# Transposes of the identity in pairs 1 to 4, and another PSUM bank for the last 64 queries' second scores

## The chip, the cores and the metric

One core of one Trainium2 chip runs the whole program. The metric is the device time of one execution in microseconds (us). Three executions of the kernel before took 951.35, 951.52 and 954.31 us, a median of 951.52 us. The profile is of one more execution, which took 954.08 us; its span, from the first to the last instruction, is 952.4 us.

## What is computed

An attention layer is followed by two feed-forward layers. Cut to what matters here (B, H, S, D = 4, 8, 576, 64):

```python
scores = scale * np.matmul(q, k.transpose(0, 1, 3, 2))          # per batch and head, 576 x 576
scores = np.where(causal, -1e9, scores)
a = np.exp(scores - scores.max(-1, keepdims=True)); a /= a.sum(-1, keepdims=True) + 1e-9
local = np.matmul(a, v)
mem_out = (phi(q) @ M_prev) / (phi(q) . z_prev)
attn = g * mem_out + (1 - g) * local
x = relu(attn @ w_in) ** 2 @ w_out                              # 2304 tokens, 512 -> 2048 -> 512
out = gate[token] * relu(x @ w1[e]) @ w2[e]                     # e: the token's best of 8 experts
```

## The kernel before

The attention walks over 16 pairs (a batch and two heads). A pair has nine units, in the order of `ORDER`: unit 0 is the last 64 queries of both heads (576 keys), units 1 to 8 are the four blocks of 128 queries of head 0 and head 1, in the row order 3, 0, 2, 1. One loop (L611) counts units through all pairs: `t = 9 * pair + i`. In its turn `t` the loop issues, for TensorE in exactly this order, since TensorE's order is the written one (L1458):

- `busy(n)` where `BUSY` lists `t`: n transposes of the identity into a tile `w`, which nobody reads;
- the products with the values (`values`, L538) of unit `t - 8`, into a tile `xo`;
- a step of the first feed-forward layer (`step`, L1445), once enough of its input is there (from pair 5 on);
- the transposes of the next pair's queries and keys (`prep`: `tk`, `tq`, `t2`, `tp`);
- the transposes of unit `t - 5`'s probabilities (`turn`, L500);
- the scores of unit `t` (`scores`, L446), which end in a PSUM tile `ps`.

VectorE masks the scores of unit `t` and takes their maximum in turn `t + 1` (L480, called the reduction below); ScalarE then exponentiates, VectorE inverts the sums (L489 to L495), GpSimd scales (L434, L437). VectorE and GpSimd also convert the feed-forward weights from the float64 bits that DMAs bring (L117), a few operations in nearly every turn, so that VectorE's line holds much that is not attention. Up to turn 71 VectorE's and GpSimd's orders are the written ones too.

PSUM banks: `psS` has two, in turn, for the scores. Unit 0 needs more than a bank's 512 columns and takes two tiles, 320 columns and 256 columns; the second is called the second scores below. `psX` has one bank: `xo`, the sum over the values of a pair's first 512 queries, is opened in the fifth unit of the next pair (i = 5), closed in i = 8, and copied out by ScalarE (L585) in the turn after. `busy` also uses `psX`; before the change it runs only in turns -5 to 7, where no `xo` is open. A tile in a bank can be written only when the bank's earlier tile has been read.

Of the kernel before, what the change touches and what calls it, by code (L numbers as in the profile page):

```python
# [9 lines left out]
F32 = DT.float32  # L10
# [11 lines left out]
B, H, S, D = 4, 8, 576, 64  # L22
# [34 lines left out]
START, EARLY, MIX = (3, 2, 1), 5, 1  # L57

FREE = 72
STRICT, BUSY = 9, {-5: 14, 0: 12, 2: 6, 4: 4, 5: 4, 6: 4, 7: 4}  # L60


TURN0, TURN1 = 5, 3
# [124 lines left out]
def attention(tc, sh, q, k, v, M, z, beta, w_in, w_out, mlp, step):  # L188

    nc = tc.nc  # L190
    with ExitStack() as ctx:
        c = ctx.enter_context(tc.tile_pool(name="ac", bufs=1))
        st = ctx.enter_context(tc.tile_pool(name="ast", bufs=2))
        psS = ctx.enter_context(tc.tile_pool(name="psS", bufs=2, space=PSUM))
        psT = ctx.enter_context(tc.tile_pool(name="psT", bufs=2, space=PSUM))
        psX = ctx.enter_context(tc.tile_pool(name="psX", bufs=1, space=PSUM))
# [39 lines left out]
        def load(p):  # L236
            b, hp = divmod(p, NPP)
            qn_, kn_ = naturals.get(p, (qn, kn))
            fetch(p, (k, kn_), (q, qn_))
            zb = st.tile([128, 128], F32, name="zb", tag="zb")  # L240
            nc.sync.dma_start(zb, z[b:b + 1, 2 * hp:2 * hp + 2].rearrange("o h d -> o (h d)").to_broadcast([128, 128]))
            nat[p] = (vns[p % 3], zb, Mts[p % 3], qn_, kn_)
# [8 lines left out]
        def fetch(p, *pairs):  # L251
            b, hp = divmod(p, NPP)
            for src, t in pairs:
                eng = nc.scalar if p == 0 and src is q else nc.sync
                for h in range(2):
                    eng.dma_start(t[:, 0:4, h * 64:h * 64 + 64],
                                      src[b, 2 * hp + h, 0:512].rearrange("(c p) d -> p c d", p=128))
                eng.dma_start(t[:64, 4].rearrange("p (h d) -> p h d", h=2),
                                  src[b, 2 * hp:2 * hp + 2, 512:576].rearrange("h p d -> p h d"))
# [159 lines left out]
        def new_S(b):  # L419
            if b == 0:  # L420
                turns[0] += 1
                if turns[0] % 3 == 0:
                    return sh.psm.tile([128, 512], F32, name="ps", tag="L1", bufs=1)
            return psS.tile([128, 512], F32, name="ps", tag="S")
# [4 lines left out]
        def scale(p, h, r, n, a, b):  # L429

            if p < NPP:
                d = diag[p, h, r] = diags[:, made[0] % 8 * 128:made[0] % 8 * 128 + 128]
                made[0] += 1
                nc.gpsimd.tensor_scalar(d, ident, a, b, ALU.mult, ALU.mult)  # L434
            else:
                A = soft[p, h, r][:, :n]
                nc.gpsimd.tensor_scalar(A, A, a, b, ALU.mult, ALU.mult)  # L437
# [8 lines left out]
        def scores(p, h, r):  # L446

            qs, ks, hq, lq, hk, kl = state[p][:6]
            qz = state[p][8]
            b, hp = divmod(p, NPP)  # L450
            A = A8 if h is None else st.tile([128, 512 if r > 1 else 256], F32, name="A", tag="A" if r > 1 else "As",
                                              bufs=NA if r > 1 else NAS)
            nm = st.tile([128, 2], F32, name="nm", tag="nm", bufs=5)
            if h == 1:
                sm = sums.pop((p, r))
            else:
                sm = sums[p, r] = st.tile([128, 2], F32, name="sm", tag="sm", bufs=5)
            soft[p, h, r] = A
            if h is None:
                n = S  # L460
                parts = [(0, 320, 320), (320, 256, 256)]
                terms = [(qb[0], hk), (qb[1], hk), (qb[0], kl)]
            else:
                n = 128 * (r + 1)
                parts = [(0, n, max(n, 256))]
                rows, half = slice(r * 128, r * 128 + 128), slice(h * 64, h * 64 + 64)
                if p:
                    terms = [(qs[:, h, rows], ks[:, h]), (qz[:, h, rows], kl)]
                else:
                    terms = [(hq[half, rows], hk[half]), (lq[half, rows], hk[half]), (hq[half, rows], kl[half])]  # L470
            tiles = []
            for a, w, wide in parts:
                ps = new_S(b)
                tiles.append(ps)
                for j, (x, y) in enumerate(terms):
                    nc.tensor.matmul(ps[:, :wide], x, y[:, a:a + wide], start=j == 0, stop=j == len(terms) - 1)  # L476
            yield
            for j, (a, w, _) in enumerate(parts):
                end = 768 if h is not None else 256 if j else 576
                nc.vector.tensor_tensor_reduce(A[:, a:a + w], tiles[j][:, :w], mask[:, end - w:end], -1.0, 3e38,  # L480
                                               ALU.add, ALU.min, nm[:, j:j + 1])
            if len(parts) > 1:
                nc.vector.scalar_tensor_tensor(nm[:, 0:1], nm[:, 0:1], 3e38, nm[:, 1:2], ALU.min, ALU.min)
            yield
            i = h or 0
            nc.scalar.activation(A[:, :n], A[:, :n], AF.Exp, bias=nm[:, 0:1], scale=-1.0, accum_out=sm[:, i:i + 1])  # L486
            yield
            if h is None:
                nc.vector.scalar_tensor_tensor(sm[:, 0:1], sm[:, 0:1], 1e-9, mask[:, 0:1], ALU.add, ALU.add)  # L489
                nc.vector.reciprocal(sm[:, 0:1], sm[:, 0:1])  # L490
                sums.pop((p, r))
                scale(p, h, r, n, sm[:, 0:1], g2[:, hp:hp + 1])
            elif h:
                nc.vector.scalar_tensor_tensor(sm, sm, 1e-9, mask[:, 0:2], ALU.add, ALU.add)
                nc.vector.reciprocal(sm, sm)  # L495
                for i in range(2):
                    scale(p, i, r, n, sm[:, i:i + 1], g1[:, 2 * hp + i:2 * hp + i + 1])
            yield
# [101 lines left out]
        def due(eng):  # L600
            for f in queue.pop((t, eng), ()):
                f()

        def busy(n):

            w = psX.tile([128, 512], F32, name="w", tag="X")
            for _ in range(n):
                nc.tensor.transpose(w[:, :128], ident, ident)

        here, before, gens, t = None, None, [prep(0)], -EARLY  # L610
        while t < len(units) + LP + 5 or queue:  # L611
            now[0] = t
            p, i = divmod(t, 9)
            if t == STRICT:
                strict.close()
                strict.enter_context(tc.manual_schedule(engines={ENG.DVE, ENG.Pool}))
            if t == FREE:
                strict.close()
            if t in BUSY:
                busy(BUSY[t])  # L620
            start = START[min(p, 2)]
            if 0 <= p < NPAIR - 1 and i == start:
                gens.append(prep(p + 1))
            for d, x in evacs:
                nc.scalar.copy(d, x)
            evacs.clear()
            due("act0")
            if here is not None:
                next(here)
            due("dve0")  # L630
            with then(ENG.Activation):
                if here is not None:
                    next(here)
            with then(ENG.DVE):
                if before is not None:
                    next(before)
            before, here = here, None
            if t == MIX:
                mix()
            if t == AHEAD:  # L640
                next(conv)
            due("act")
            with then(ENG.DVE):
                due("dve")
            due("pool")
            if t > CONV[0] and t % 9 != CONV[1] and next(conv, conv) is not conv:
                sh.converted += 1
            n = t - LP
            if n % 9 == 0 and (n - 1) // 9 in JOINED:
                values(*units[n - 1])  # L650
            if 0 <= n < len(units) and (n % 9 < 8 or n // 9 not in JOINED):
                values(*units[n])
            if 0 <= p < NPAIR - 2 and i == 8:
                load_values(p + 2)
            if t % 9 != REST:
                step(t)
            for g in list(gens):
                if next(g, gens) is gens:
                    gens.remove(g)
            if 0 <= p < NPAIR - 2 and i == start + 5:  # L660
                load(p + 2)
            if 0 <= t - LT < len(units):
                turn(*units[t - LT])
            if 0 <= t < len(units):
                here = scores(*units[t])
                next(here)
            for f in behind_scores:
                f()
            behind_scores.clear()
            t += 1  # L670
# [852 lines left out]
```

## Time and profile before

| what | value |
|---|---|
| median of three executions | 951.52 us |
| the profiled execution | 954.08 us |
| its span | 952.4 us |
| TensorE busy, share of the span | 904.4 us, 95% |
| VectorE busy | 599.2 us, 63% |
| ScalarE busy | 527.8 us, 55% |
| GpSimd busy | 293.3 us, 31% |

The shares hide two stages. Up to about 180 us the pairs 0 to 7 of the attention run, with VectorE, ScalarE, GpSimd and the DMAs all well used, and TensorE has gaps. From there to the end TensorE is busy nearly throughout. The page of the profile gives the granted clock of TensorE in tenths for each fortieth of the span; the view by windows gives it for any stretch. The timeline gives each instruction's start and length, and in brackets how long its engine stood idle before it and which event ended that.

### The profile page before, as it was taken

How to read it: one execution, taken by the hardware profiler on the slowest of the kernel's cores; microseconds unless marked ns; L12 is line 12 of the kernel's file. 1: busy time of each engine (PE TensorE's matmuls, PEld its weight loads, DVE VectorE, ACT ScalarE, POOL GpSimd, SP SyncE). 2: the span in 40 equal slices, each digit the busy share in tenths (PEclk: the TensorE clock that was granted, in tenths of full speed). 3: DMA queues.
4: the chain of work that ended last, by engine and by line, in shares of the span. 5: the costliest groups of instructions: out<-in, count | busy, mean ns of one | idle time of the engine just before them, and what ended most of it. 6: DMA issues, size and time to landing. Idle time of an engine off the chain costs nothing.

```text
span 952.4 us, 19267 instructions
## 1 busy us (share of the span) xinstructions
PE 904.4 (95%) x6319; PEld 791.8 (83%) x6319; DVE 599.2 (63%) x1737; ACT 527.8 (55%) x1363; POOL 293.3 (31%) x356
## 2 busy tenths in 40 slices
PE   7887689999999999999999999999999999999993
PEld 5766578788888888898888888888899999999983
DVE  4688878655565654587527778889762535353551
ACT  4677777777676767576655555665421424242440
POOL 4455657534334443000311111432311311111111
PEclk9989999999999999999999999999999999999997
DMA  7666666544444420144311112411060635252521
GB/s 175 151 165 166 148 156 147 114 119 101 118 111 108 108 64 23 69 156 153 117 62 39 52 45 89 167 67 54 26 222 24 203 104 169 94 179 89 187 70 35
DMA packets 107081, 105.81 MB, mean 111 GB/s; under 512 B 66095, under 2 KB 76335, under 8 KB 106944
## 3 DMA queue, kind: packets, MB, share of 16 engines
q1 hardware_dynamic: 100528, 89.13, 33.7%
q0 software_dynamic: 4544, 13.67, 4.4%
q10 hardware_dynamic: 1872, 1.34, 0.5%
q8 instruction: 66, 1.08, 0.5%
q14 instruction: 71, 0.58, 0.2%
HBM read 70.80 MB, written 14.70 MB: 90 GB/s over the span
## 4 chain that ended last, share of the span: by engine, by line
PE 72%; issue 5%; DVE 5%; DMA 3%; ACT 1%; POOL 1%; SPq 0%; POOLq 0%; DVEq 0%; ACTq 0%
PE ps L751 18%; PE psh L1318 11%; PE y L785 6%; PE y L787 6%; PE y L786 6%; PE ps L476 4%; PE xo L570 3%; PE psy L1334 3%; PE psy L1336 3%; PE psy L1335 3%; PE pt L442 3%; DMA raw<-in_moe_w_in_dram 1%; DMA raw<-in_moe_w_out_dram 1%; PE xo L549 1%; DVE wt L146 1%
## 5 line engine op out<-in xcount | busy, mean ns | idle before, releaser
L480 DVE CUSTOM_DVE_ANT_0 A<-ps,mask 128x256 f32<-128x256 f32 (+4 forms) x160 | 75.5, 480 | 96.6 <-PE ps L476 95.2
L751 PE MATMUL ps<-xh,Wh 128*128 128x256 f32 x416 | 119.0, 286 | 0.1
L437 POOL TENSOR_SCALAR A<-A,sm,g 128x512 f32<-128x512 f32 (+4 forms) x108 | 81.3, 759 | 121.7 <-DVE sm L495 76.8
L751 PE MATMUL ps<-xl,Wh 128*128 128x256 f32 x416 | 118.3, 284 | 0.0
L751 PE MATMUL ps<-xh,Wl 128*128 128x256 f32 x416 | 118.0, 284 | 0.0
L785 PE MATMUL y<-Wh,gh 128*128 128x512 f32 x288 | 115.6, 401 | 0.0
L787 PE MATMUL y<-Wh,gl 128*128 128x512 f32 x288 | 113.6, 394 | 1.3 <-DVE es L1046 1.1
L486 ACT ACTIVATE A<-A,nm 128x576 f32<-128x576 f32 (+2 forms) x144 | 84.6, 588 | 53.6 <-DVE nm L480 26.6
L786 PE MATMUL y<-Wl,gh 128*128 128x512 f32 x288 | 113.4, 394 | 0.0
L1320 ACT ACTIVATE hh<-psh 128x512 fp32r<-128x512 f32 x44 | 26.4, 599 | 144.4 <-PE psh L1318 72.7
L1318 PE MATMUL psh<-xTh,Wh 128*128 128x256 f32 x352 | 99.2, 282 | 0.9 <-PEq L1326 0.7
L755 ACT ACTIVATE r<-ps 128x256 f32<-128x256 f32 x144 | 55.1, 383 | 80.0 <-PE ps L751 69.7
L1318 PE MATMUL psh<-xTh,Wl 128*128 128x256 f32 x352 | 98.8, 281 | 0.2 <-DVE Wl L114 0.2
L1318 PE MATMUL psh<-xTl,Wh 128*128 128x256 f32 x352 | 98.7, 280 | 0.0
L761 DVE TENSOR_TENSOR gl<-r,gh 128x256 fp32r<-128x256 f32 x144 | 71.0, 494 | 33.4 <-ACT gh L760 32.9
L1321 DVE SCALAR_TENSOR_TENSOR hl<-psh,hh 128x512 fp32r<-128x512 f32 x44 | 30.4, 690 | 93.0 <-ACTq L1308 38.1
L751 PEld LDWEIGHTS ps<-xh,Wh 128*128 128x128 f32 x416 | 79.8, 192 | 3.4 <-ACT r L755 0.5
L751 PEld LDWEIGHTS ps<-xl,Wh 128*128 128x128 f32 x416 | 79.8, 192 | 3.1 <-DVE xl L729 0.2
L751 PEld LDWEIGHTS ps<-xh,Wl 128*128 128x128 f32 x416 | 79.8, 192 | 0.0
L760 ACT CAST gh<-r 128x256 fp32r<-128x256 f32 x144 | 58.3, 405 | 33.7 <-PE y L786 31.3
L1318 PEld LDWEIGHTS psh<-xTh,Wh 128*128 128x128 f32 x352 | 66.2, 188 | 2.6 <-ACTq L1308 1.1
L1334 PE MATMUL psy<-Wh,hh 128*128 128x512 f32 x168 | 67.1, 399 | 0.1
(348 smaller groups left out, 2418.5 us busy)
## 6 DMA issues: line engine op xcount, KB each, us to landing
x<-in_moe_w_dram SPq DMA_DIRECT2D x48, 512.0 KB, 4.2
ks<-hk SPq DMA_DIRECT2D x60, 128.0 KB, 2.4
raw<-in_moe_w_in_dram SPq DMA_DIRECT2D x15, 512.0 KB, 3.8
raw<-in_moe_w_out_dram SPq DMA_DIRECT2D x15, 512.0 KB, 3.7
x2d<-x SPq DMA_DIRECT2D x18, 256.0 KB, 2.0
vn<-in_v_dram SPq DMA_DIRECT2D x32, 128.0 KB, 3.2
x2p<-x SPq DMA_DIRECT2D x16, 256.0 KB, 3.0
part<-x2p SPq DMA_DIRECT2D x16, 256.0 KB, 2.9
```

The lines of the kernel that those rows point to most:

```text
L437: nc.gpsimd.tensor_scalar(A, A, a, b, ALU.mult, ALU.mult)
L480: nc.vector.tensor_tensor_reduce(A[:, a:a + w], tiles[j][:, :w], mask[:, end - w:end], -1.0, 3e38, ALU.add, ALU.min, nm[:, j:j + 1])
L486: nc.scalar.activation(A[:, :n], A[:, :n], AF.Exp, bias=nm[:, 0:1], scale=-1.0, accum_out=sm[:, i:i + 1])
L751: nc.tensor.matmul(ps[:, :CH], a, b, start=n == 0, stop=n == len(ops) - 1)
L755: self.later(1, "act", lambda: nc.scalar.activation(r, ps[:, :CH], AF.Relu))
L760: self.later(3, "act", lambda: nc.scalar.copy(gh, r))
L761: self.later(3, "dve", lambda: nc.vector.tensor_tensor(gl, r, gh.bitcast(F32), ALU.subtract))
L785: nc.tensor.matmul(y, gh[:, sl], wh, start=first, stop=False)
L786: nc.tensor.matmul(y, gh[:, sl], wl, start=False, stop=False)
L787: nc.tensor.matmul(y, gl[:, sl], wh, start=False, stop=last)
L1318: nc.tensor.matmul(ps[:, a], w[kc][:, sl], x[:, kc], start=kc + j == 0, stop=kc + j == 5)
L1334: nc.tensor.matmul(y[h], xh, wh, start=g + a == 0, stop=False)
```

## The change

- Six transposes of the identity in the turns 10 to 13, 19 to 22, 28 to 31 and 37 to 40, which are units 1 to 4 of pairs 1 to 4. They stand behind the step and `prep` and ahead of `turn` and `scores`.
- In turn 5 (unit 5 of pair 0) 18 such transposes instead of 4.
- In turn 64 (unit 1 of pair 7) 14 such transposes, behind `turn` and ahead of `scores`.
- The second scores of unit 0 go, in all pairs, into the bank of `psX` instead of one of `psS`.
- `busy` takes `psX` in the units 0 to 4 of a pair and `psS` in the others; all turns that it is called in take `psX`.

```diff
-STRICT, BUSY = 9, {-5: 14, 0: 12, 2: 6, 4: 4, 5: 4, 6: 4, 7: 4}
+STRICT, BUSY = 9, {-5: 14, 0: 12, 2: 6, 4: 4, 5: 18, 6: 4, 7: 4}
+TURNS = {t: 6 for t in range(10, 45) if 0 < t % 9 < 5}
+SCORES = {64: 14}
...
-                ps = new_S(b)
+                ps = psX.tile([128, 512], F32, name="ps", tag="X") if a else new_S(b)
...
-            w = psX.tile([128, 512], F32, name="w", tag="X")
+            pool, tag = (psX, "X") if t < 9 or t % 9 < 5 else (psS, "S")
+            w = pool.tile([128, 512], F32, name="w", tag=tag)
             for _ in range(n):
                 nc.tensor.transpose(w[:, :128], ident, ident)
...
                 load(p + 2)
+            if t in TURNS:
+                busy(TURNS[t])
             if 0 <= t - LT < len(units):
                 turn(*units[t - LT])
+            if t in SCORES:
+                busy(SCORES[t])
             if 0 <= t < len(units):
                 here = scores(*units[t])
```

## Rows read from the trace of the kernel before

**Rows 1.** The page: the span, and the granted clock in forty slices

```profile
span 952.4 us, 19267 instructions
...
PEclk9989999999999999999999999999999999999997
```

**Rows 2.** Windows: length; busy PE, PEld, DVE, ACT, POOL (instructions); clock; DMA; GB/s

```profile
0.00:30.00 30.00, 24.07 (x150) 19.29 (x150) 12.85 (x45) 14.52 (x37) 12.05 (x36) 0.89 0.70 169
51.22:58.28 7.06, 3.57 (x24) 2.97 (x23) 6.86 (x21) 5.32 (x12) 4.24 (x6) 0.90 0.49 127
58.28:66.80 8.52, 8.52 (x46) 6.24 (x47) 5.09 (x16) 4.49 (x14) 3.24 (x4) 0.68 0.73 196
73.69:80.81 7.12, 3.26 (x20) 2.51 (x21) 6.95 (x21) 4.68 (x12) 4.48 (x6) 0.99 0.50 123
80.81:88.70 7.89, 7.89 (x49) 6.45 (x49) 5.19 (x16) 6.34 (x18) 4.10 (x5) 0.79 0.67 180
101.32:104.80 3.48, 3.48 (x15) 2.99 (x16) 1.64 (x7) 1.78 (x4) 2.26 (x2) 0.52 0.52 113
125.25:128.60 3.35, 3.35 (x14) 3.15 (x15) 1.44 (x4) 1.23 (x4) 2.07 (x2) 0.51 0.90 253
169.66:173.10 3.44, 3.44 (x15) 3.25 (x16) 2.66 (x10) 2.17 (x6) 2.95 (x6) 0.53 0.82 183
180.00:390.00 210.00, 210.00 (x1645) 181.40 (x1642) 119.33 (x422) 146.93 (x428) 80.11 (x98) 1.00 0.38 90
```

**Rows 3.** Timeline of TensorE, pair 0: start, length, operation [idle before <-releaser]

```profile
1.69 3.25 PE L608 MATMUL w<-ident 128*128 128x128 f32 x14 [1.69 <-POOL ident masks.py:199]
...
6.51 1.47 PE L608 MATMUL w<-ident 128*128 128x128 f32 x12
...
15.18 0.66 PE L608 MATMUL w<-ident 128*128 128x128 f32 x4
18.08 0.66 PE L403 MATMUL tp<-ident,e 128*128 128x128 f32 x4 [2.25 <-POOL e L396]
...
21.14 0.79 PE L444 MATMUL pt<-x,A 128*128 128x128 f32 x2 [1.32 <-ACT AT L625]
```

**Rows 4.** Timeline of ScalarE, pair 1's weights and pair 3's copies

```profile
43.26 0.66 ACT L139 ACTIVATE wt<-raw 128x512 f32<-128x512 f32 x1 [0.90 <-DMA raw<-in_moe_w_in_dram]
...
92.60 0.65 ACT L585 COPY x<-xo 128x256 f32<-128x256 f32 x2
```

**Rows 5.** Timeline of VectorE: reductions of second scores in pairs 2, 3, 4, 7; 88.73: pair 3

```profile
53.98 0.41 DVE L480 CUSTOM_DVE_ANT_0 A<-ps,mask 128x256 f32<-128x256 f32 x1
...
77.64 0.41 DVE L480 CUSTOM_DVE_ANT_0 A<-ps,mask 128x256 f32<-128x256 f32 x1
...
88.73 0.56 DVE L480 CUSTOM_DVE_ANT_0 A<-ps,mask 128x384 f32<-128x384 f32 x1 [2.63 <-PE ps L476]
...
98.64 0.42 DVE L480 CUSTOM_DVE_ANT_0 A<-ps,mask 128x256 f32<-128x256 f32 x1
...
169.51 0.42 DVE L480 CUSTOM_DVE_ANT_0 A<-ps,mask 128x256 f32<-128x256 f32 x1
```

**Rows 6.** Timeline of TensorE, pairs 1 to 7: where it waited

```profile
44.54 1.13 PE L444 MATMUL pt<-x,A 128*128 128x128 f32 x8 [2.60 <-POOL x L434]
...
50.62 0.60 PE L322 MATMUL tk<-ident,x 128*128 128x128 f32 x4
...
58.28 1.09 PE L403 MATMUL tp<-ident,e 128*128 128x128 f32 x4 [3.19 <-DVE sm L489]
...
73.09 0.60 PE L322 MATMUL tk<-ident,kn 128*128 128x128 f32 x4
...
80.81 1.08 PE L403 MATMUL tp<-ident,e 128*128 128x128 f32 x4 [2.30 <-DVE kl L324]
...
95.90 0.38 PE L476 MATMUL ps<-hk,qbh 128*128 128x256 f32 x1 [1.59 <-DVE nm L480]
...
118.86 0.38 PE L476 MATMUL ps<-hk,qbh 128*128 128x256 f32 x1 [2.01 <-DVE nm L480]
...
169.66 0.80 PE L476 MATMUL ps<-ks,qs 128*128 128x512 f32 x1 [2.05 <-DVE nm L480]
```

## Prediction, made before the changed kernel was run

> **What bounds the kernel now.** I read the page first, for the slices of the granted clock [rows 1]: they are at 9 nearly throughout, with one 8 early on, so a loss of clock is small and lies in few places. Then the windows by stage [rows 2]. From 180 to 390 us TensorE is busy for all of 210.00 us at clock 1.00. Whatever happens earlier therefore only shifts this part, and the end moves by what the time at 180 us moves. So the question is the first 180 us, pairs 0 to 7, and there the finer windows and the timelines.
>
> The reader is to see a pattern in [rows 2]. In pair 2 TensorE is busy for only 3.57 of the 7.06 us from 51.22 to 58.28, while VectorE is busy for 6.86; in the next 8.52 us TensorE is busy all the time, but at a mean clock of 0.68, and VectorE for only 5.09. Pair 3 has the same: 3.26 of 7.12 us, then 7.89 us all busy at clock 0.79. First VectorE holds TensorE up; the clock falls to its lower level (1.2 GHz) after the gap; then TensorE at that level holds VectorE up, as its 2.63 us of idle time at 88.73 shows [rows 5]. Shorter stretches at about 0.52 follow the gaps of pairs 4, 5 and 7 [rows 2]. Pair 0 has one too: the clock's mean over the first 30 us is 0.89 [rows 2].
>
> **What half the clock costs.** A busy stretch of length L at a mean clock c would take L times c at full clock, so it costs L(1 - c). Pair 2: 8.52 x 0.32 = 2.7 us. Pair 3: 7.89 x 0.21 = 1.7. Pair 4: 3.48 x 0.48 = 1.7. Pair 5: 3.35 x 0.49 = 1.6. Pair 7: 3.44 x 0.47 = 1.6 [rows 2]. In pair 0, 30 us x 0.11 is 3.3 us of lost clock, of which the 2 us or so of idle time in that stretch cost nothing at that clock: TensorE's busy part of it, from 21.14 on, comes to about 4.9 us at half clock, 2.4 us lost. These are the sums that the transposes could win back, 11.7 us together.
>
> **What one transpose costs.** At the full clock twelve take 1.47 us with the last one's drain of 0.27, so 0.11 us each; the first fourteen took 3.25 us, 0.23 each, the pace of the lower level [rows 3]. Six cost 0.66 us, fourteen 1.54 us; at the lower level twice that. In all 96 + 14 + 14 = 124 are added, 13.6 us of TensorE at full clock. They are free only where TensorE would have waited.
>
> **Pair 0: 14 more in turn 5.** Their place is behind 15.18, ahead of the `tp` that waits 2.25 us for GpSimd [rows 3]. 1.54 us fits in there, so they delay nothing, and 0.7 us of the gap is left. What follows, at 21.14, waits for ScalarE whatever TensorE does. From there TensorE goes without a gap; at full clock it would be 2.4 us ahead at the end. Bounds: 0 (the clock falls all the same, for the wait of 1.32 us at 21.14) and -2.4. I take -2.4, since the larger gap of the two is filled.
>
> **Pair 1: 4 x 6.** 2.64 us of transposes stand in a stretch where TensorE has work; behind it there is a wait of 2.60 us [rows 6], which is named for GpSimd, but whose chain is ScalarE, which waited for a DMA of weights (0.90 us at 43.26) before it could empty the banks [rows 4]. The clock is not low here, so there is nothing to win. The wait covers most; the DMA that it hangs on cannot come forward by the whole 2.4 us won in pair 0. Bounds 0 and +2.64; I take +1.0.
>
> **The gate.** The main point is the bank. After the change the second scores of unit 0 lie in `psX`, and the first six transposes, in unit 1, write `psX`. They must wait until VectorE has reduced those scores, and behind them on TensorE, in its written order, wait `turn` and the scores of units 1 to 4. Before, TensorE ran ahead here: it did `tk` at 50.62, and then units 1 and 2 before it stopped. The reduction ends at 54.39 in pair 2, at 78.05 in pair 3, at 99.06 in pair 4, at 169.93 in pair 7 [rows 5]. So TensorE will stop earlier and for longer: from 51.2 to 54.4 in pair 2 (3.2 us) and from 73.7 to 78.05 in pair 3 (4.4 us). Gaps of 2 to 3 us were followed by the lower clock in pairs 2, 3 and 7 [rows 2, 6], so I expect it at the gate too. The transposes come behind this gap, not in it.
>
> Pair 2: from 54.4, TensorE has the 3.57 us that it did before between 51.22 and 58.28, 18 transposes (2.0 us), and some 2.4 us at half clock (1.2 us lost). `tp` comes at 61.2 instead of 58.28: +2.9. From there the clock is full: -2.7. Six transposes of unit 4 stand behind `tp`, in a stretch that TensorE bounds: +0.66. Together +0.8 (rounded).
>
> Pair 3: 78.05 + 3.26 + 12 transposes (1.3) + 1.4 lost at half clock = 84.0, against 80.81: +3.1. Then -1.7 for the clock, and +1.3 for the twelve behind `tp`. Together +2.7.
>
> Pair 4: the gate opens at 99.06; six transposes, `turn` and the scores of unit 1 follow, partly at half clock, and end about 1.0 us later than before. The 1.7 us of clock come back from 101.32 on, less 0.66 for unit 2's transposes. Together 0.
>
> **The second scores in their new bank.** They no longer wait for a bank of `psS`: 1.59 us in pair 4 and 2.01 us in pair 5 go [rows 6]. But VectorE, which they wait for, does not get faster, and its line is what the next waits hang on. `xo` must be copied out first: in pair 4 that was at 92.60 to 93.25 [rows 4], ahead of the earliest start of these scores. So 0 for the wait itself. In pair 5, which has no transposes, the gap ahead of 125.25 moves, and with it perhaps the 1.6 us: between -1.6 and +1.6, I take -0.4. In the later pairs TensorE is busy throughout [rows 2] and has no wait to lose.
>
> **Pair 7: 14 in turn 64.** Before, the scores of unit 1 waited 2.05 us for the reduction of the first scores, and started at 169.66 [rows 6]. In the new bank they would not wait; but the 14 transposes ahead of them wait for the reduction of the second ones, 169.93, and take 1.54 us, or 3.1 at half clock. Scores at 171.5 instead of 169.66 is +1.8, less 1.6 if the clock is up by then: +0.2. At half clock throughout it is +1.8 (the scores come 3.4 us later, and the 1.6 comes back afterwards). I take +0.3.
>
> **Sum.** -2.4 + 1.0 + 0.8 + 2.7 + 0 - 0.4 + 0.3 = +2.0 us. Against the profiled execution (954.08 us, of which 952.4 are the span [rows 1]) that is 956.1; it is 2.6 us above the median of 951.52, so in terms of the median I forecast 953.5 us. About 0.3%, 2.85 us, is what a measurement of this kernel can tell from no change; the forecast is within that.
>
> **A rule against the change.** Transposes alone: the fourteen at 1.69 ran at 0.23 us apiece and the twelve at 6.51 at 0.11, with nothing but other transposes in between [rows 3], so here the clock rose while TensorE did transposes only. The Trainium skill, "TensorE: Matmul & The Clock Gate", Part 4 (PE-mode transpose), says that transposes do not count as busy for the clock in the same way. By that rule the added ones would keep no clock up, pair 0's 2.4 us would not come, and the sum would be +4.4. The row speaks against it, so it gets a small chance.
>
> **Rivals.** (a) *The clock holds.* If VectorE's reduction of the second scores comes early enough that the transposes fill the gaps rather than follow them, the clock stays up: pairs 2, 3, 4 and 7 win 2.7 + 1.7 + 1.7 + 1.6 = 7.7 us and pay for the transposes that nothing covers, 0.66, 1.3, 0.66 and 0.5: -4.6. With pairs 0 and 1 that is -6.0, 945.5 us; with one or two pairs held, about 948. For it: the gaps are of nearly the size that the transposes fill. Against it: VectorE is busy for 6.86 of 7.06 us and 6.95 of 7.12 us there [rows 2], and its order is fixed, so the reductions cannot come early. (b) *The gate costs more, slower.* The place is unit 1 of pairs 4 and 7 and what follows in pair 5. If the clock is low there too when the gate opens, and stays so, pair 4 pays 1.7, pair 5 0.7 and pair 7 1.8 instead of 0, -0.4 and 0.3: +6.3 in all, 957.8 us. It decides from the point where the gap ahead of the gate is as long as the 2.05 us that pair 7 already has. For it: the gaps get longer; against it: the stretch of 1.59 us in pair 4 was not followed by a lower clock. (c) *Transposes don't keep the clock up*: +4.4, 955.9 us, by the paragraph above. (d) *The bank does nothing else but move a wait, and pair 0 wins*: -1.4, inside the forecast's own range.
>
> **Chances.** The forecast, within 0.3% of no change: 0.40, its own range 949 to 954.3. Rival (a) 0.28. Rival (b) 0.26, (c) 0.06. Faster by over 0.3%: 0.28; within: 0.40; slower: 0.32. The range reaches to both sides, 946 to 957.5, since the cost of the gate and the fall of the clock are each open by some 1.6 us per pair.
>
> **What would show it.** Right: in the changed kernel's timeline the first transposes of turns 19, 28 and 37 start as VectorE's second reduction ends, after 3 to 4 us of idle time, at a granted clock of 0.5; the clock is 1.00 from 10 to 30 us; the weights' wait of pair 1 is shorter. The start of pair 8 (about 190 us) moves by the whole difference. Wrong: the first six start without a wait, or the clock stays at 1.00 through 50 to 110 us; then (a) holds. If the clock still falls near 20 us, pair 0's term is wrong, and (c) comes up.

## Result and profile after

| kernel | median | lowest to highest | ratio to before, 95% interval |
|---|---|---|---|
| before, 4 executions | 952.91 us | 951.35 to 956.49 | |
| after, 4 executions | 964.17 us | 958.93 to 966.2 | 1.0102 [1.0066, 1.0138] |

The change makes the kernel slower by 11.3 us, 1.0%. The forecast, 953.5 us, was too low and its range, up to 957.5, too short. The profiled execution of after took 962.51 us, 8.4 more than that of before; the other 2.8 us lie in executions without a trace.

First the page of after, which answers to [rows 1]: the span, the busy times and the clock in forty slices.

```profile
span 960.8 us, 19535 instructions
...
PE 914.1 (95%) x6443; PEld 804.8 (84%) x6443; DVE 596.3 (62%) x1737; ACT 528.0 (55%) x1363; POOL 294.6 (31%) x356
...
PEclk9898899999999999999999999999999999999997
```

TensorE is busy for 914.1 us instead of 904.4, and three slices in the first 120 us show an 8, where before had one. Then the windows of after, with the columns of [rows 2].

```profile
0.00:30.00 30.00, 24.25 (x133) 20.00 (x134) 11.90 (x40) 13.35 (x33) 11.92 (x35) 0.90 0.68 166
58.61:62.00 3.39, 3.39 (x17) 3.26 (x18) 2.38 (x9) 1.35 (x3) 2.18 (x3) 0.59 0.16 34
82.94:89.60 6.66, 6.66 (x32) 6.32 (x33) 3.42 (x11) 3.32 (x8) 3.39 (x4) 0.57 0.34 76
107.17:113.00 5.83, 5.83 (x27) 5.39 (x28) 3.79 (x12) 2.56 (x7) 2.00 (x4) 0.53 0.56 157
116.00:144.00 28.00, 22.33 (x185) 17.46 (x184) 22.61 (x69) 21.74 (x61) 16.70 (x17) 1.00 0.67 168
180.00:390.00 210.00, 210.00 (x1646) 181.92 (x1646) 123.03 (x437) 151.86 (x444) 85.04 (x104) 1.00 0.40 93
```

The last line is that of before: TensorE without a gap, at full clock. So the whole loss lies ahead of 180 us. The other lines show the low clock still there, in new places: behind 58.61, 82.94 and 107.17 us. What stands at those three times is in the timeline of TensorE in after.

```profile
16.03 2.19 PE L611 MATMUL w<-ident 128*128 128x128 f32 x18
18.68 0.66 PE L405 MATMUL tp<-ident,e 128*128 128x128 f32 x4 [0.46 <-POOL e L398]
22.13 0.49 PE L446 MATMUL pt<-x,A 128*128 128x128 f32 x2 [1.91 <-ACT AT L628]
...
33.48 0.39 PE L478 MATMUL ps<-hk,qbh 128*128 128x320 f32 x1
...
58.61 1.54 PE L611 MATMUL w<-ident 128*128 128x128 f32 x6 [3.23 <-DVE nm L482]
...
82.94 1.54 PE L611 MATMUL w<-ident 128*128 128x128 f32 x6 [5.03 <-DVE nm L482]
...
107.17 1.54 PE L611 MATMUL w<-ident 128*128 128x128 f32 x6 [3.38 <-DVE nm L482]
...
178.24 1.75 PE L611 MATMUL w<-ident 128*128 128x128 f32 x14 [2.40 <-DVE nm L482]
...
200.21 0.39 PE L478 MATMUL ps<-hk,qbh 128*128 128x320 f32 x1
```

It is the gate of the prediction: the point where the first transposes of a pair wait until VectorE has read the bank that they write. The first six transposes of pairs 2, 3 and 4 wait 3.23, 5.03 and 3.38 us for VectorE's reduction (L482 here, L480 before), and then run at the lower clock: 1.54 us for six, where 0.82 is the time at full clock. Before, the scores and `tp` waited there instead, for 1.59 to 3.19 us [rows 6].

The start of a pair's first scores (the `ps<-hk,qbh` of 320 columns) in the two traces, pairs 1 to 8, gives each pair's length. Of before, the lines of pairs 1 and 8 (those of after stand above):

```profile
31.06 0.39 PE L476 MATMUL ps<-hk,qbh 128*128 128x320 f32 x1
...
191.58 0.39 PE L476 MATMUL ps<-hk,qbh 128*128 128x320 f32 x1
```

| pair | 0 | 1 | 2 | 3 | 4 | 5 | 6 | 7 | sum |
|---|---|---|---|---|---|---|---|---|---|
| next pair starts, before | 31.06 | 49.61 | 71.86 | 93.63 | 116.16 | 144.37 | 165.67 | 191.58 | |
| next pair starts, after | 33.48 | 53.77 | 76.43 | 102.31 | 127.07 | 152.83 | 173.91 | 200.21 | |
| change of its length | +2.4 | +1.7 | +0.4 | +4.1 | +2.2 | -2.5 | -0.2 | +0.4 | +8.6 |
| forecast | -2.4 | +1.0 | +0.8 | +2.7 | 0 | -0.4 | 0 | +0.3 | +2.0 |

This compares one trace with one trace. Pairs 2 to 4 together take 66.6 us in the trace of before (49.61 to 116.16) and 73.3 in that of after. Of the traces of the experiments below, the two with transposes in units 1 to 4 behind a gate (bank_gate_one_rest and bank_and_turns) have 71.5 and 71.7 us there, and the other thirteen 61.1 to 66.8.

At last the waits that lie between TensorE and VectorE, from 50 to 116 us: engine, what waited, for whom; us in total, times, longest. Before:

```profile
DVE A L480 <- PE ps L476: 6.7, 3, 2.6
PE ps L476 <- DVE nm L480: 3.8, 4, 1.6
PE tp L403 <- DVE sm L489: 3.2, 1, 3.2
...
PE tp L403 <- DVE kl L324: 2.3, 1, 2.3
```

and after:

```profile
DVE A L482 <- PE ps L478: 15.2, 8, 3.4
PE w L611 <- DVE nm L482: 11.6, 3, 5.0
```

TensorE waited 9.3 us (3.8 + 3.2 + 2.3) and now waits 11.6, all of it at the gate: little more. But VectorE, for which TensorE then is late, waits 15.2 us for scores instead of 6.7, and 8.5 us more is of the size of what the kernel lost. From 50 to 116 us after is not as far on as before; over the whole of pairs 2 to 4 (49.61 to 116.16 and 53.77 to 127.07 us) VectorE's two sums are 6.7 and 16.4. The two engines now wait for each other in turn.

### The profile page after: what moved, and what is told of

The parts are those of the page before. It is cut to its first block, busy times and chain, and to the rows that moved or that the text cites. A ratio compares the mean times of both kernels' runs of the same rounds, so it can differ in the third digit from the quotient of the medians.

```text
span 960.8 us, 19535 instructions
## 1 busy us (share of the span) xinstructions
PE 914.1 (95%) x6443; PEld 804.8 (84%) x6443; DVE 596.3 (62%) x1737; ACT 528.0 (55%) x1363; POOL 294.6 (31%) x356
## 4 chain that ended last, share of the span: by engine, by line
PE 76%; DVE 10%; issue 6%; DMA 4%; ACT 1%; POOL 1%; SPq 1%; POOLq 0%; DVEq 0%; ACTq 0%
PE ps L758 19%; PE psh L1325 11%; PE y L792 7%; PE y L794 6%; PE y L793 6%; PE ps L478 4%; PE psy L1343 3%; PE psy L1341 3%; PE xo L572 3%; PE psy L1342 3%; PE pt L444 3%; DVE A L482 2%; DMA raw<-in_moe_w_out_dram 2%; DMA raw<-in_moe_w_in_dram 1%; DVE x L895 1%
## 5 line engine op out<-in xcount | busy, mean ns | idle before, releaser
L482 DVE CUSTOM_DVE_ANT_0 A<-ps,mask 128x256 f32<-128x256 f32 (+4 forms) x160 | 75.6, 480 | 111.3 <-PE ps L478 109.9
```

## The experiments

The change has four parts: the bank of the second scores, the transposes in units 1 to 4, those in turn 64, and those in turn 5. Two theories stood against each other. **The wait**: the gate itself costs, since it stops TensorE and lets the clock fall. **The lead**: the gate alone costs nothing; it takes away the units that TensorE was ahead of VectorE, and from then on every transpose behind it is paid for in full. The short diffs are against the kernel before; of those that have `TURNS` or `SCORES`, the lines that call `busy` are shown once each.

### One part alone

```diff
# bank_alone
-                ps = new_S(b)
+                ps = psX.tile([128, 512], F32, name="ps", tag="X") if a else new_S(b)
# turns_alone
+TURNS = {t: 6 for t in range(10, 45) if 0 < t % 9 < 5}
...
+            if t in TURNS:
+                busy(TURNS[t])
# bank_and_turns: both of these
# turn5_alone
-STRICT, BUSY = 9, {-5: 14, 0: 12, 2: 6, 4: 4, 5: 4, 6: 4, 7: 4}
+STRICT, BUSY = 9, {-5: 14, 0: 12, 2: 6, 4: 4, 5: 18, 6: 4, 7: 4}
```

Bank alone:

> The second scores of unit 0 in the values' bank, nothing else of the change; no transposes added. Gate theory (the loss comes from the first six transposes of a pair, which wait for the reduction of these scores): within 2 us of before, since nothing waits on that bank early; the waits of 1.59 us and 2.01 us in pairs 4 and 5 go. Rival, the bank itself or the other order that it gives ScalarE costs the time: 5 us or more slower.

96 transposes alone, the second scores in their old bank, so that no transpose waits for them:

> The 96 transposes of pairs 1 to 4, with the second scores left in their old banks, so that the transposes wait for nothing. Gate theory: within 3 us of before, either way, since they stand in TensorE's gaps, and pairs 2 to 4 lose less of the clock. Rival, the transposes' own time (96 x 0.11 = 10.6 us) and the changed order on ScalarE are the loss: 6 us or more slower, with no TensorE wait ahead of the transposes of unit 1.

Both:

> Both of the two parts, without the transposes of turns 5 and 64. Gate theory: 6 to 10 us slower, about what the whole change is (+11 us in the medians), with TensorE waits of 3 to 5 us ahead of the transposes of turns 19, 28 and 37. Rival: the sum of the two parts alone.

Turn 5 alone:

> Only the 14 more transposes in turn 5. As forecast: 2.4 us faster, if the clock stays up in pair 0 after 19 us. As the changed kernel's trace suggests, where the clock fell at about 24 us all the same: within 1 us of before, with the stretch at the lower clock moved and not gone.

| kernel | median, us | ratio to before, 95% interval |
|---|---|---|
| before | 953.21 | |
| bank_alone | 950.38 | 0.998 [0.9954, 1.0006] |
| turns_alone | 955.34 | 1.0039 [1.0016, 1.0063] |
| bank_and_turns | 961.09 | 1.0093 [1.006, 1.0127] |
| turn5_alone | 954.48 | 1.0014 [0.9988, 1.004] |

Bank and transposes together make nearly the whole loss, and it is not the sum of the two: -0.2% and +0.39% are +0.19%, and together they cost 0.93%. Neither part does it; their meeting does.

### The gate with one transpose, with six, and without

```diff
# bank_gate_one: the bank, and one transpose in unit 1 of pairs 1 to 4
+TURNS = {t: 1 for t in range(10, 45) if t % 9 == 1}
# bank_gate_six: the bank, and six there
+TURNS = {t: 6 for t in range(10, 45) if t % 9 == 1}
# bank_units2to4: the bank, and six in units 2, 3 and 4, none in unit 1
+TURNS = {t: 6 for t in range(10, 45) if 1 < t % 9 < 5}
# bank_gate_one_rest: the bank, one in unit 1, six in units 2, 3 and 4
+TURNS = {t: 1 if t % 9 == 1 else 6 for t in range(10, 45) if 0 < t % 9 < 5}
```

> The new bank, and a single transpose in unit 1 of pairs 1 to 4: four in all, 0.44 us of TensorE, but the same wait. Gate theory: the wait itself costs; 3 to 7 us slower than the bank alone, so 1 to 5 us slower than before. Rival, the work of the transposes behind the wait is what costs: within 1 us of the bank alone.

> The new bank and six transposes in unit 1 alone (24, all behind the wait). Theory of the lost lead: the wait takes away TensorE's lead over VectorE, which costs nothing by itself; then every transpose behind it delays the pair by its own time, 0.11 to 0.23 us. Six a pair: 3 to 4 us above the bank alone, so 1 to 3 us slower than before. Rival, the first six do all the harm, by keeping the clock down: 6 us or more slower than before.

> The new bank, and the six transposes only in units 2 to 4 of pairs 1 to 4 (72 instead of 96), so that none of them waits for the reduction of the second scores. Gate theory: the interaction goes, 0 to 4 us slower than before (what the transposes alone cost, 0.4%, less a quarter, less what the bank wins). Rival, bank and transposes disturb each other in some other way: still 6 us or more slower.

> The new bank, one transpose in unit 1 and six in each of units 2 to 4 (76). Theory of the lost lead: 18 transposes of 0.11 us behind the wait in each of pairs 2 to 4, about 6 us above the bank alone, so 3 to 5 us slower than before, and clearly more than the 0.2% of the same without the one that waits. Rival, the first six do the harm: as without them, within 2 us of before.

| kernel | transposes | median, us | ratio to before, 95% interval |
|---|---|---|---|
| bank_gate_one | 4 | 951.08 (before 951.67) | 0.9983 [0.9959, 1.0006] |
| bank_gate_six | 24 | 953.98 (before 952.43) | 1.0019 [0.9996, 1.0042] |
| bank_units2to4 | 72 | 953.71 (before 951.67) | 1.0018 [0.9996, 1.0039] |
| bank_gate_one_rest | 76 | 957.9 (before 952.43) | 1.0054 [1.0032, 1.0077] |

One transpose keeps most of the wait, as the timeline of TensorE in bank_gate_one shows:

```profile
53.95 0.33 PE L609 MATMUL w<-ident 128*128 128x128 f32 x1 [2.17 <-DVE nm L481]
...
74.85 0.33 PE L609 MATMUL w<-ident 128*128 128x128 f32 x1 [3.56 <-DVE nm L481]
...
95.63 0.40 PE L609 MATMUL w<-ident 128*128 128x128 f32 x1 [3.06 <-DVE nm L481]
```

and yet the kernel is as fast as with the bank alone. The first theory falls: the wait itself costs nothing that can be measured. In these traces it costs no clock either: added up over windows of half a microsecond (TensorE's busy time times what the clock lacks of 1), pairs 2 to 4 lose 5.0 us in bank_gate_one and 4.9 in bank_alone. The waits from 50 to 116 us of bank_gate_one

```profile
PE w L609 <- DVE nm L481: 8.8, 3, 3.6
DVE A L481 <- PE ps L477: 5.6, 6, 2.1
```

against those of bank_and_turns

```profile
DVE A L481 <- PE ps L477: 14.4, 7, 3.4
PE w L609 <- DVE nm L481: 11.3, 3, 4.7
```

say where the price is: TensorE waits at the gate in both, but VectorE waits 5.6 us for scores in the one and 14.4 in the other. bank_gate_six and bank_gate_one_rest lie between them, at 9.2 and 12.0; bank_units2to4 has 11.9 too, but 6.2 of it in a single wait. The 72 transposes of units 2 to 4 show it in the time: without a transpose in unit 1 +0.18%, behind a gate of one transpose +0.54%. In the first of these the bank still makes a few of them wait, though less, and not in every pair, as the timeline of bank_units2to4 shows for pairs 2 and 3:

```profile
61.85 0.87 PE L609 MATMUL w<-ident 128*128 128x128 f32 x6 [0.58 <-DVE nm L481]
...
83.48 0.88 PE L609 MATMUL w<-ident 128*128 128x128 f32 x6 [1.83 <-DVE nm L481]
```

The stretch in which it happens, pair 3 from the opened gate to the first product with the values, as windows of bank_gate_one

```profile
74.85:81.27 6.42, 6.42 (x38) 5.99 (x39) 5.28 (x16) 4.56 (x10) 3.70 (x5) 0.73 0.22 47
```

of bank_and_turns

```profile
84.31:92.95 8.64, 8.63 (x62) 8.35 (x63) 6.43 (x21) 6.09 (x15) 3.68 (x5) 0.84 0.53 141
```

and of after

```profile
82.94:93.03 10.09, 10.09 (x62) 9.63 (x63) 6.42 (x21) 6.06 (x15) 3.69 (x5) 0.71 0.48 121
```

TensorE is busy in all of it in each, so its length is work plus lost clock. Length times clock is the work at full clock: 6.42 x 0.73 = 4.7 us, 8.63 x 0.84 = 7.2, 10.09 x 0.71 = 7.2. The 23 further transposes are 23 x 0.11 = 2.5 us, the whole of the step from 4.7 to 7.2: in this stretch not one of them is hidden. The rest is the clock: 1.7, 1.4 and 2.9 us lost. How long the low clock lasts behind the gate varies from trace to trace, by a factor of two in the same stretch.

### Where transposes are free

```diff
# turns_units1and2: old bank; units 1 and 2 of pairs 2 to 4
+TURNS = {t: 6 for t in (19, 20, 28, 29, 37, 38)}
# turns_units3and4: old bank; units 3 and 4 of pairs 2 to 4
+TURNS = {t: 6 for t in (21, 22, 30, 31, 39, 40)}
```

> No new bank; six transposes in units 1 and 2 of pairs 2 to 4 only (36), ahead of TensorE's long waits and behind no wait of their own. If the transposes cost where TensorE bounds (pair 1, and units 3 and 4, behind the waits) and keep the clock up where it waits: 1 to 4 us faster than before. If what they win in clock is not on the path at all: within 1 us of before.

> No new bank; six transposes in units 3 and 4 of pairs 2 to 4 only (36). Where TensorE bounds: 2 to 4 us slower than before (36 x 0.11 = 4.0 us, less some clock). With the 0.3% that the same number in units 1 and 2 won, this tells apart a transpose ahead of TensorE's wait and one behind it.

Units 1 and 2 gave 949.25 us against 951.67, 0.9969 [0.9949, 0.9988]; units 3 and 4 gave 953.64 against 952.43, 1.0019 [0.9995, 1.0043]. The first is faster than both kernels, with the same six a turn that the change has, in the old bank. Its timeline of TensorE in pair 3:

```profile
72.20 0.82 PE L609 MATMUL w<-ident 128*128 128x128 f32 x6
...
75.63 0.82 PE L609 MATMUL w<-ident 128*128 128x128 f32 x6
...
78.45 0.63 PE L404 MATMUL tp<-ident,e 128*128 128x128 f32 x4 [0.87 <-DVE kl L325]
```

and its windows over pairs 2 and 3:

```profile
50.00:72.00 22.00, 18.98 (x176) 16.49 (x173) 19.37 (x63) 17.96 (x51) 12.13 (x14) 1.00 0.75 179
72.00:94.00 22.00, 17.86 (x155) 14.66 (x154) 19.30 (x55) 16.44 (x47) 14.97 (x18) 1.00 0.76 180
```

In before the same stretches have

```profile
50.00:72.00 22.00, 18.51 (x137) 14.89 (x138) 18.08 (x51) 15.76 (x43) 11.96 (x15) 0.84 0.72 179
72.00:94.00 22.00, 18.05 (x140) 14.87 (x140) 18.89 (x54) 16.10 (x44) 12.90 (x14) 0.92 0.67 170
```

The transposes wait for nothing and stand ahead of the wait of `tp`, which was 2.30 us [rows 6] and is 0.87. All of TensorE's idle time from the start of pair 3 to its `tp` falls from 3.9 us to 1.8; in turns_alone, with the same twelve transposes there, to 3.0, so a part of that differs from trace to trace. The clock of 1.00 in one trace doesn't settle it either, for the trace of turns_units3and4 has 1.00 in both stretches too:

```profile
50.00:72.00 22.00, 18.74 (x160) 15.72 (x158) 19.83 (x59) 17.07 (x48) 12.54 (x15) 1.00 0.73 180
72.00:94.00 22.00, 17.62 (x154) 14.85 (x155) 19.09 (x57) 17.29 (x47) 14.70 (x17) 1.00 0.71 178
```

What tells the two places apart is the time, and the mean clock of twelve executions: 0.9870 with units 1 and 2, 0.9805 with units 3 and 4, 0.9813 before. Of units 3 and 4, the six of unit 3 in pair 2 still stand ahead of `tp`'s wait; in pairs 3 and 4 both sixes come when it is over. That they cost there because TensorE bounds is argued and not shown; their +0.19% holds 0.

### Turn 64

```diff
# scores64_alone: old bank, 14 transposes in turn 64
+SCORES = {64: 14}
...
+            if t in SCORES:
+                busy(SCORES[t])
# bank_scores64: the same with the bank
# bank_scores64_one: the bank, and SCORES = {64: 1}
```

> The 14 transposes of turn 64 without the new bank, so that they wait for nothing and stand in the 2.05 us that TensorE waits there anyway. If the wait in front of them is what cost 0.8% with the bank: within 1.5 us of before, or up to 1.6 us faster where the clock stays up in pair 7. If their own time costs: 1.5 us or more slower.

> The new bank and the 14 transposes of turn 64. They wait about 2.4 us for the reduction of pair 7's second scores and then take 1.5 us at full clock, ahead of scores that could have started: 1 to 3 us slower than the bank alone, so within 2 us of before. If the clock's fall in pair 7 is what they prevent: 1 us or more faster than the bank alone.

> The new bank and a single transpose in turn 64, ahead of the scores: the wait of 2.4 us without the work behind it. If the wait is what costs in pair 7, as it holds up scores that are next on the path: 4 us or more above the bank alone, so 2 us or more slower than before. If, as in pairs 2 to 4, the wait costs nothing and the 14 transposes do: within 2 us of the bank alone, so faster than before or equal.

scores64_alone 951.94 us against 952.43, 0.9994 [0.9972, 1.0016]; bank_scores64 956.32 against 951.67, 1.0062 [1.0042, 1.0082]; bank_scores64_one 952.15 against 953.5, 0.9997 [0.9971, 1.0024]. The same pattern once more: 14 that wait for nothing are free, a wait with one transpose behind it is free, and 14 behind the wait cost 0.8% against the bank alone. The timelines of TensorE show why the first is free (scores64_alone)

```profile
166.92 1.69 PE L609 MATMUL w<-ident 128*128 128x128 f32 x14
169.15 0.50 PE L477 MATMUL ps<-ks,qs 128*128 128x512 f32 x1 [0.54 <-DVE nm L481]
```

and the last is not (bank_scores64)

```profile
165.46 1.75 PE L609 MATMUL w<-ident 128*128 128x128 f32 x14 [2.40 <-DVE nm L481]
166.97 0.48 PE L477 MATMUL ps<-ks,qs 128*128 128x512 f32 x1
```

In the one the 14 fill the time before the scores may start, in the other they follow it. The size isn't explained. In this trace the pair is 1.8 us longer than in bank_alone (26.3 against 24.5), while the ratios differ by 0.8%, some 7.8 us; the traced execution, 950.55 us, was the fastest of its twelve. What the others lost, no trace shows. Nor does the whole change show this loss: it has turn 64 and turn 5 on top of bank_and_turns, and stands at 1.0102 [1.0066, 1.0138] against 1.0093 [1.006, 1.0127].

### Undoing the bank, and the best of the parts

```diff
# whole_old_bank: all transposes of the change, second scores in their old bank
                 ps = new_S(b)
# units1and2_and_64: old bank
+TURNS = {t: 6 for t in (19, 20, 28, 29, 37, 38)}
+SCORES = {64: 14}
```

> The whole change without the new bank: all 124 transposes, none of which then waits for a reduction. Theory of the lost lead: the sum of the parts alone, 0.39% + 0.14% - 0.06%, so 3 to 6 us slower than before, about half of the whole change's 1.0%. Rival, the number of transposes on TensorE is what costs: 8 us or more slower, as the whole change.

> No new bank; six transposes in units 1 and 2 of pairs 2 to 4, and 14 in turn 64: transposes only where TensorE waits anyway and where nothing makes them wait. Each part alone gave -0.31% and -0.06%; 2 to 5 us faster than before. If the part in turn 64 costs its time where the clock is up: no better than units 1 and 2 alone.

Without the bank all 124 transposes cost 0.28% (954.43 us against 953.5, 1.0028 [1.0001, 1.0054]) instead of 1.02%. The two kernels give TensorE the same work, and windows of half a microsecond over pairs 0 to 7 split the time up to pair 8 into three parts:

| trace | pair 8 starts, us | TensorE's work at full clock | lost to the clock | idle |
|---|---|---|---|---|
| before | 191.6 | 149.7 | 12.0 | 29.9 |
| whole_old_bank | 191.6 | 163.7 | 6.6 | 21.3 |
| after | 200.2 | 161.8 | 10.1 | 28.3 |

In these traces idle time and lost clock pay for the transposes with the old bank; with the new one nearly all of them come on top. (The trace of whole_old_bank is 2.3 us longer than that of before all the same, behind the start of pair 8.)

units1and2_and_64 gave 949.14 against 953.5, 0.9967 [0.9943, 0.9991]: no better than turns_units1and2, within the intervals.

### What the clock has to do with it

Each execution comes with its mean granted clock. The 134 executions of the kernel before that were made beside these runs took 943.2 to 957.9 us, at clocks from 0.990 down to 0.974; a straight line through them falls by 7.8 us for each 0.01 of clock, and they scatter about it by 1.5 us (standard deviation). It goes through 952.3 us at 0.9813. For each kernel, the mean over its executions then splits into what its clock gives by that line and what is left at equal clock. It is a split by correlation, not a measurement of a cause.

| kernel | mean clock | by the clock, us | left at equal clock, us |
|---|---|---|---|
| after (4 executions; the others 12) | 0.9785 | +2.2 | +8.9 |
| bank_alone | 0.9819 | -0.5 | -1.0 |
| bank_gate_one | 0.9823 | -0.8 | -1.0 |
| bank_gate_six | 0.9786 | +2.1 | -0.7 |
| bank_units2to4 | 0.9826 | -1.0 | +2.9 |
| bank_and_turns | 0.9812 | +0.1 | +8.1 |
| bank_gate_one_rest | 0.9808 | +0.4 | +5.3 |
| turns_alone | 0.9837 | -1.9 | +4.6 |
| whole_old_bank | 0.9847 | -2.6 | +5.7 |
| turn5_alone | 0.9812 | +0.1 | +1.8 |
| turns_units1and2 | 0.9870 | -4.5 | +1.4 |
| turns_units3and4 | 0.9805 | +0.6 | +1.5 |
| scores64_alone | 0.9816 | -0.2 | -0.7 |
| bank_scores64 | 0.9802 | +0.9 | +3.5 |
| bank_scores64_one | 0.9804 | +0.7 | -0.7 |
| units1and2_and_64 | 0.9873 | -4.7 | +2.1 |

In the old bank the four kernels with transposes in units 1 and 2 buy clock, 2 to 5 us of it; those of units 3 and 4 and of turn 64 alone buy next to none. Behind the gate none is bought. The mean of bank_and_turns is some 5.5 us above that of turns_alone: by this split 2.0 of them are clock and 3.5 are left at equal clock, so the new bank costs both. In bank_gate_six the whole of the loss goes with the clock.

## Why the prediction was right or wrong

**The bound, and where to look: right.** The stretch from 180 us on is the same; pair 8 starts 8.6 us later, and the span is 8.4 us longer.

**The gate: right in place, wait and clock; its price was not.** Turns 19, 28 and 37 start as the reduction ends, after 3.23, 5.03 and 3.38 us of idle time, at the lower clock. The Trainium skill, "Perfetto Trace Analysis", Optimizing Tensor Performance (Matmuls), says that independent groups of matmuls should rotate through PSUM banks, so that the engines that empty one overlap with the next group. The transposes were put into the bank that VectorE had yet to read, and bank_and_turns against turns_alone, 961.09 against 955.34 us, agrees.

**Pair 0, -2.4: wrong, +2.4 measured.** Its step was that what follows at 21.14 us then runs at full clock, since the larger gap is filled. The gap ahead of `tp` did shrink, from 2.25 us [rows 3] to 0.46, but the wait for ScalarE behind it grew from 1.32 to 1.91 us, and the clock over 30 us is 0.90, no better than 0.89. (The prediction's 2 us or so of idle time in that window are 5.9, 30.00 less 24.07; its 2.4 us lost holds, for from 21.14 to 31.06 the clock is 0.75.) The 2.4 us were read off one trace: in those of turns_alone and turns_units1and2, whose pair 0 is that of before, the clock over the same 30 us is 1.00, and pair 0 ends at 29.2 and 28.9 us. The bound of 0 should have been taken: the prediction had that second wait in its hand. Whether the 14 cost something here is open. Pair 0 ends between 28.9 and 34.1 us in the 17 traces, and all three with this edit are at 33.5 to 34.1, but so are three without it; the time of turn5_alone says +0.14% [-0.12%, +0.40%], which leaves no room for 2.4 us, 0.25%, won.

**Pair 1, +1.0: +1.7 measured**, inside its bounds. The long wait did shrink, from 2.60 us [rows 6] to 0.89.

**Pair 2, +0.8: +0.4 measured.** The sum held: from 58.61 to 62.00 us the clock is 0.59, a loss of 1.4 us, where 1.2 had been taken.

**Pair 3, +2.7: +4.1 measured.** The term that was too small is the low clock behind the gate, taken at 1.4 us. From the gate to `tp`, the 6.66 us at 0.57 lose 6.66 x 0.43 = 2.9 us.

**Pair 4, 0: +2.2 measured.** The step that failed is "the 1.7 us of clock come back". They were replaced: 5.83 us at 0.53 lose 2.7. Rival (b) had this pair pay, at 1.7.

**Pair 5, -0.4: -2.5 measured**, outside its bounds of 1.6 either way. From 116 to 144 us the clock is 1.00, where it was 0.51 for 3.35 us from 125.25 [rows 2]; these 1.6 us came back whole, and 0.8 of idle time went as well.

**Pair 7, +0.3: +0.4 measured** in the trace, by the way that was forecast: the 14 wait 2.40 us, take 1.75 at the full clock, and the 1.6 of clock come back, as the window of after shows:

```profile
178.24:183.00 4.76, 4.76 (x38) 4.58 (x39) 2.10 (x8) 3.02 (x9) 3.21 (x6) 1.00 0.45 98
```

With the bank alone beside it, turn 64 costs some 0.8% over many executions, more than the prediction's bound of +1.8 us; in the whole change no such loss is seen.

**The step that failed** is that the clock comes back and pays for the transposes. The sum charges most of them (1.0, 2.7, 2.6 and some 1.7 us in pairs 1 to 4) and sets against them clock won back: 2.4 us in pair 0, 2.7 less 1.2 in pair 2, 1.7 less 1.4 in pair 3, 1.7 in pair 4, 1.5 in pair 7. By the table of the three traces above, from before to after TensorE's work up to pair 8 grows by 12.1 us, while the clock lost falls by 1.8 and the idle time by 1.6: hardly any transpose is hidden, and little clock comes back. In pairs 2 to 4, where the sum won 3.5 us of clock, 1.0 more is lost than before (6.0 us before, 7.0 after).

The step missing in the sum is what the gate does to work behind it. The runs show that the wait alone is free, and that what has a price is the work put behind it: once TensorE has no unit in hand, its 2.6 us of transposes a pair (24 x 0.11) delay the scores, VectorE waits for them, and the next gate opens later. Against bank_alone the 96 transposes of bank_and_turns cost 1.13% by the ratios, 10.8 us, and 96 x 0.11 is 10.6.

**The rivals.** (a) is out: the clock fell in pairs 2 to 4. (b), 957.8 us, had the right sign, and pair 4 right, but not pairs 5 and 7; and a gap of 2.05 us isn't what decides, since pair 7's gate of 2.40 us was followed by the full clock, while one of 2.17 (pair 2 of bank_gate_one) had 0.61 over the next 4 us. (c), that transposes don't keep the clock up, is contradicted by the mean clock of turns_units1and2, 0.9870 against 0.9813, and by the rise at the start of the trace [rows 3]. So the rule of the Trainium skill that the prediction weighed ("TensorE: Matmul & The Clock Gate", Part 4) does not hold for these fp32 transposes. (d) is out with pair 0, and by the time.

**What stays open.** Three things have no cause yet: that the clock falls in pair 0 in some traces and not in others, the 2.8 us by which the medians differ more than the profiles, and the size of turn 64's loss. The bank alone, taken at 0, is -0.2% with an interval that holds 0. ScalarE's and SyncE's orders are planned by a scheduler, not written in the program, and are not the same in all these kernels. Up to 200 us, ScalarE's differs from that of before in 9 places in bank_alone, 40 in turns_alone and 49 in bank_and_turns, while VectorE's is the same in all three. This wasn't held fixed, and what share of the differences comes from it is not shown.

## What to carry to other kernels

Work that only keeps an engine awake was free here ahead of a wait that was there anyway, and cost about its full time behind one that it had made itself; so look first at what its operands and, above all, its output bank wait for. An in-order engine's lead over the engine it feeds is a store that hides added work; a new wait that costs nothing by itself may empty that store, and then price both edits together, not one by one. When two gaps follow one another, filling the larger may just lengthen the other.

## What the runs showed of the hardware

Six transposes take 1.54 us at the lower clock and 0.82 at the full one. 36 of them, placed ahead of waits, raised the mean clock of twelve executions from 0.9813 to 0.9870; the same number elsewhere left it at 0.9805.

The length of a gap did not by itself say whether the low clock follows: 2.40 us were followed by 1.00 (178.24 us in after), 2.05 by 0.53 (169.66 us in before) and 2.17 by 0.61 (53.95 us in bank_gate_one). Behind a gate of the same kind the low clock lost 1.4 us in one trace and 2.9 in another, in the same stretch of the same work.

The same kernel, unchanged, took 943.2 to 957.9 us from one execution to the next, and most of that went with its mean clock. One profile of the first 30 us says little on an edit there: with the same pair 0, that pair ends at 28.9 us in turns_units1and2 and at 32.1 in scores64_alone.
